# One of the gate's products done as seven smaller ones instead of eight, over two weight pairs and two token pairs, in the first two weight groups

## The chip, the cores and the metric

The kernel runs on one core of a Trainium2 chip. A run's time is the device time in microseconds (us) from launch to end. TensorE (PE in the profile, its weight loads PEld) does the matmuls, VectorE (DVE) and ScalarE (ACT) the elementwise work, GpSimd (POOL) some of it and some DMA issues, SyncE (SP) issues most DMAs. TensorE writes its sums to PSUM, which has 8 banks; a bank holds 512 fp32 numbers in each of 128 partitions.

## The reference, cut to what matters

```python
def reference(A_x, A_w1, A_b1, A_w2, A_b2, B_x, B_w_gate, B_w_up, B_w_down, gate_w):
    x = A_x                                                  # 2 x 1 x 4096 x 640
    g = sigmoid((x * gate_w).sum(-1, keepdims=True))
    a = _A_ref(x, A_w1, A_b1, A_w2, A_b2)                    # spectral mixing: rfft2, block MLP, irfft2
    b = (gelu(x @ B_w_gate) * (x @ B_w_up)) @ B_w_down       # 640 -> 1728 -> 640
    return g * a + (1 - g) * b
```

All of it is fp32. The change concerns `gelu(x @ B_w_gate) * (x @ B_w_up)`, for 8192 tokens, 640 channels and 1728 hidden columns.

## The kernel before, in words

**Precision.** Each fp32 operand is split into a high and a low part (`high` on ScalarE, `low` on VectorE), both of type float32r, and a product is three matmuls: high x high, high x low, low x high (`prod`). The helper `run` issues a list of such matmuls into one PSUM target.

**Tiling.** The hidden columns are cut into 13 full weight pairs `t` of 128 gate and 128 up columns, and a rest. The tokens are cut into 16 token pairs `tp`; each holds a first and a second half of 256 tokens. The 640 channels are a first half b1x (256, two matrices of 128), a second half b2x (256) and 128 more, k4. So `b21` is the second channel half of the first token half, and `g2` the gate's weights for the second channel half.

**The quad.** For one `tp` and one `t`, `quad` computes gate and up for both token halves with a seven-product scheme (g1 b11, g2 b21, s1 t1, s2 t2, s3 t3, s4 b22, u2 t4; t1 to t4 and s1 to s4 are sums of tokens and of weights). Its running sums: bank `X` starts with g1 b11 and is copied by ScalarE to `p1`; bank `C` takes s3 t3; bank `A` takes g2 b21, 6 matmuls, and VectorE adds it to p1 (L525), which is the gate of the first token half. X goes on with s2 t2 (copied to `u2`), and the quad's second part, three functions in the queue `Q`, runs between the products of the next quad: s1 t1 on X (`u4`, and gelu of p1 on ScalarE), s4 b22 on X (gelu to `h`), u2 t4 on C (added to u2 at L551). Then VectorE multiplies gate and up (L553, L554) and h is stored to `hD`.

**Order.** Weight pairs come in three groups: 0 to 3, 4 to 7, 8 to 13. `keys` lists (group, token pair) in the order of work, and for each key the quads of the group follow each other; in the second group token pair 0 comes fifth. `manual_schedule` keeps the order of the code on each engine. Other work is put between the products by a table: `slots[(i, q)]` is run by the `hook` calls of key number i, seven a quad, and `todo` after a quad. By it go the weights of the next group (`w_raw` loads, `w_prep` makes sums and splits), the tokens of the next key (`x_raw`, `x_prep`), and the first step of the spectral branch (`a_split`, `a_gate`, `a_step`), whose matmuls (L645) stand between those of the quads. In the first group `x_prep` makes t1 to t4 and keeps them in memory (`xD`, stored by GpSimd); in later groups they are loaded from there.

**Buffers.** Tiles come from tagged pools of fixed size (`big`, `mid`, `small`, `tiny`, 8 PSUM banks); an instruction that writes a tile waits until the slot's earlier users are done. Semaphores are set by the framework: readers and writers of one PSUM bank are kept apart whichever columns they touch.

Of the kernel before, what the change touches and what calls it, by code (L numbers as in the profile page):

```python
# [23 lines left out]
CW = CH + 2  # L24
NCH = 8
NPAIR = 13

# [186 lines left out]
def spectral_mix_kernel(ctx: ExitStack, tc: tile.TileContext, a):  # L214
# [36 lines left out]
    def st(dst, src):  # L251
        late.append((dst, src))
# [10 lines left out]
    hD = dram.tile([64, P, 14 * P], F32, name="hD")  # L263
    wdf = [dram.tile([P, 13 * 320], F32, name=f"wdf_{j}") for j in range(7)]
    wdl = dram.tile([P, 7 * 320], F32, name="wdl")

    fny = consts.tile([P, 8], F32, name="fny")
    sgn = consts.tile([P, 4], F32, name="sgn")
# [33 lines left out]


    WG, XT, XO, RAW = {}, {}, {}, {}

    def w_raw(t):
        RAW[t] = []
# [5 lines left out]
    def w_prep(t, plain=False):  # L313


        o = {}

        def gate_high():
            o["r"] = RAW.pop(t)
            o["w0"] = big([P, 5, 2, P], F32R, name="w0")  # L320
            high(o["w0"][:, :, 0], o["r"][0])

        def up_high():
            o["w1"] = big([P, 5, 2, P], F32R, name="w1")
            high(o["w1"][:, :, 0], o["r"][1])

        def up_low():
            low(o["w1"][:, :, 1], o["r"][1], o["w1"][:, :, 0])
            WG[t] = o["w0"], o["w1"]

        def st0():
            if not plain:
                gate_high()
            if t < NPAIR:
# [60 lines left out]
        def piece(ks):  # L395
            if "r" not in o:
                o["r"] = RAW.pop(t)
                o["w0"], o["w1"] = (big([P, 5, 2, P], F32R, name=f"w{k}") for k in range(2))
                WG[t] = o["w0"], o["w1"]
            for w, r in zip(WG[t], o["r"]):  # L400
                high(w[:, ks, 0], r[:, ks])
            for w, r in zip(WG[t], o["r"]):
                low(w[:, ks, 1], r[:, ks], w[:, ks, 0])
        if plain:
            if t == 0:
                return [piece, st0, st1, st3, st4, st5, st6, st7]
            return [gate_high, st2, up_high, up_low, st0, st1, st3, st4, st5, st6, st7]
        return [st0, st1, st2, st3, st4, st5, st6, st7] if t < NPAIR else [gate_high, st2]

    made = lambda key: key[0] == 0 or key == (1, 0)

    def x_raw(key, names=("b11", "b21", "b12", "b22", "k4")):
        d = XT.setdefault(key, {})
        for n in names:
            if key[0] != 1 or made(key) or n != "b12":
# [8 lines left out]
    def x_prep(key, k, eng=nc.vector):  # L426
# [35 lines left out]
        def lo():  # L462
# [7 lines left out]
        return [src, hi, lo]  # L470

    def prod(ws, x):

# [29 lines left out]
    def quad(key, t, hook):  # L503


        o, w = XO[key], WG[t]
        half = lambda: bank()[:, :256]
        T = lambda n: tiny([P, 256], name=n)
        copy = lambda d, s_: nc.scalar.activation(d, s_, AF.Copy)  # L509
        gelu = lambda d, s_: nc.scalar.activation(d, s_, AF.Gelu_apprx_tanh)  # L510
        old = Q.pop() if Q else [lambda: None] * 3

        X = half()
        run(X, prod(w["g1"], x_of(o, "b11", ("k4", 0))))
        p1 = T("p1")
# [9 lines left out]
        nc.vector.tensor_add(p1, A, p1)  # L525
        hook(3)
        run(X, prod(w["s2"], x_of(o, "t2", "t5")), first=False)
        u2 = T("u2")
        copy(u2, X)
        hook(4)  # L530
        old[1]()
        hook(5)
        old[2]()
        hook(6)
        v = {}

        def half5():
            run(X, prod(w["s1"], x_of(o, "t1", "t5")), first=False)
            u4 = v["u4"] = T("u4")
            copy(u4, X)  # L540
            gelu(p1, p1)
            nc.vector.tensor_add(u4, C, u4)  # L542

        def half3():
            run(X, prod(w["s4"], x_of(o, "b22")), first=False)
            h = v["h"] = small([P, 512], name="h")
            gelu(h[:, 256:], X)

        def half4():
            run(C, prod(w["u2"], x_of(o, "t4")), first=False)  # L550
            nc.vector.tensor_add(u2, C, u2)  # L551
            h = v["h"]
            nc.vector.tensor_mul(h[:, 256:], h[:, 256:], v["u4"])  # L553
            nc.vector.tensor_mul(h[:, :256], u2, p1)  # L554
            h_store(key[1], t, h)
        Q.append([half5, half3, half4])

    def plain(key, t, hook):

# [840 lines left out]
        spread(0, (2, 9, 16)[k - 1], w0[k][2:4])  # L1400
    for k in range(4):
        spread(*((0, 11), (0, 20), (1, 2), (1, 10))[k], w0[k][4 if k else 1:])
    for k, (l, pb) in enumerate(((1, 0), (1, 1), (2, 0), (2, 1))):
# [187 lines left out]
```

## Time and profile before

| | before |
|---|---|
| median of 3 runs | 2538.85 us (2537.32 to 2540.7) |
| the profiled execution | 2535.42 us |
| its span, first to last instruction | 2533.7 us |
| TensorE busy | 2527.2 us (100%), granted clock 1.00 |
| VectorE busy | 2052.9 us (81%) |
| ScalarE busy | 1492.7 us (59%) |
| GpSimd busy | 372.4 us (15%) |
| DMA | 483.77 MB, mean 191 GB/s |

Busy times are sums over the span; which stage they belong to is read from windows. A matmul's record overlaps the next one's, so TensorE's busy share says that it never stood idle, not that it ran at its peak. In a group's row stand: line, engine, operation, tiles as out<-in, shapes, count, then busy us and mean ns of one, then the idle time of the engine just before. In a row of the timeline stand: start, length, engine, line, operation, tiles, count, and in brackets the engine's idle time before it and what ended it.

### The profile page before, as it was taken

How to read it: one execution, taken by the hardware profiler on the slowest of the kernel's cores; microseconds unless marked ns; L12 is line 12 of the kernel's file. 1: busy time of each engine (PE TensorE's matmuls, PEld its weight loads, DVE VectorE, ACT ScalarE, POOL GpSimd, SP SyncE). 2: the span in 40 equal slices, each digit the busy share in tenths (PEclk: the TensorE clock that was granted, in tenths of full speed). 3: DMA queues.
4: the chain of work that ended last, by engine and by line, in shares of the span. 5: the costliest groups of instructions: out<-in, count | busy, mean ns of one | idle time of the engine just before them, and what ended most of it. 6: DMA issues, size and time to landing. Idle time of an engine off the chain costs nothing.

```text
span 2533.7 us, 54552 instructions
## 1 busy us (share of the span) xinstructions
PE 2527.2 (100%) x20299; PEld 2522.9 (100%) x20299; DVE 2052.9 (81%) x4218; ACT 1492.7 (59%) x3494; POOL 372.4 (15%) x379
## 2 busy tenths in 40 slices
PE   9999999999999999999999999999999999999999
PEld 9999999999999999999999999999999999999999
DVE  7878767777777767766667788888999999899998
ACT  6655555666665655655556788787644444444443
POOL 0000000000000000000003111111133333333332
PEclk9999999999999999999999999999999999999999
DMA  6566647676767677766767354548744444344432
GB/s 231 195 214 197 212 169 234 203 240 210 223 204 253 192 227 226 232 219 209 225 224 229 121 166 141 169 144 263 288 146 150 156 157 139 134 151 157 154 130 103
DMA packets 345982, 483.77 MB, mean 191 GB/s; under 512 B 24748, under 2 KB 221996, under 8 KB 345716
## 3 DMA queue, kind: packets, MB, share of 16 engines
q1 hardware_dynamic: 330884, 438.47, 54.2%
q0 software_dynamic: 14832, 41.82, 4.6%
q8 instruction: 160, 2.62, 0.4%
q14 instruction: 106, 0.87, 0.1%
HBM read 300.55 MB, written 179.64 MB: 190 GB/s over the span
## 4 chain that ended last, share of the span: by engine, by line
PE 96%; DVE 2%; DMA 1%; ACT 1%; issue 0%; SPq 0%; DVEq 0%; ACTq 0%
PE bank L483 54%; PE bank L1234 22%; PE bank L295 14%; PE bank L811 3%; PE bank L645 1%; PE bank L892 1%; PE bank L893 1%; DMA wraw<-in_wgu_dram 0%; DVE w L279 0%; DVE xo L279 0%; PE bank L894 0%; DVE xd L441 0%; DMA xraw<-in_xT_dram 0%; DVE uu L1239 0%; DVE h L554 0%
## 5 line engine op out<-in xcount | busy, mean ns | idle before, releaser
L483 PE MATMUL bank<-xo,w 128*128 128x256 f32 x11676 | 1351.0, 277 | 0.7 <-ACT u L509 0.6
L483 PEld LDWEIGHTS bank<-xo,w 128*128 128x128 f32 x11676 | 1342.2, 188 | 1.7 <-ACT u L509 1.3
L1234 PE MATMUL bank<-wx,ho 128*128 128x320 f32 x3844 | 560.6, 306 | 0.0
L1234 PEld LDWEIGHTS bank<-wx,ho 128*128 128x128 f32 x3844 | 557.1, 188 | 0.0
L509 ACT ACTIVATE u<-bank 128x256 f32<-128x256 f32 x408 | 156.6, 384 | 253.4 <-PE bank L483 248.3
L279 DVE TENSOR_TENSOR ho<-hraw,ho 128x640 fp32r<-128x640 f32 (+3 forms) x384 | 273.8, 754 | 21.4 <-ACT ho L276 18.4
L276 ACT ACTIVATE ho<-hraw 128x640 fp32r<-128x640 f32 x320 | 166.8, 571 | 91.5 <-PE bank L1234 66.0
L509 ACT ACTIVATE p<-bank 128x256 f32<-128x256 f32 x204 | 78.6, 385 | 148.4 <-PE bank L483 61.9
L279 DVE TENSOR_TENSOR xo<-xraw,xo 128x512 fp32r<-128x512 f32 x209 | 143.2, 686 | 23.9 <-ACT xo L276 23.2
L542 DVE TENSOR_TENSOR u<-bank,u 128x256 f32<-128x256 f32 x204 | 85.9, 421 | 89.2 <-ACT u L509 86.6
L279 DVE TENSOR_TENSOR xs<-xr,xs 64x640 fp32r<-64x640 f32 x128 | 104.9, 820 | 58.1 <-ACT xs L276 55.6
L295 PE MATMUL bank<-wm,h 128*128 128x320 f32 (+1 forms) x792 | 137.7, 309 | 0.0
L276 ACT ACTIVATE xo<-xraw 128x512 fp32r<-128x512 f32 x209 | 131.0, 627 | 6.1 <-DMA xraw<-in_xT_dram 4.3
L551 DVE TENSOR_TENSOR u<-bank,u 128x256 f32<-128x256 f32 x204 | 85.5, 419 | 60.0 <-PE bank L483 59.3
L647 DVE TENSOR_TENSOR as<-bank,as 64x320 f32<-64x320 f32 x256 | 113.7, 483 | 24.9 <-ACT as L646 23.7
L295 PEld LDWEIGHTS bank<-wm,h 128*128 128x128 f32 (+1 forms) x792 | 117.9, 185 | 1.4
L598 POOL MEMSET h<- 64x512 f32 x16 | 8.4, 522 | 749.8 <-PE bank L645 437.5
L483 PE MATMUL bank<-wx,ho 128*128 128x320 f32 x764 | 116.3, 307 | 0.0
L525 DVE TENSOR_TENSOR p<-bank,p 128x256 f32<-128x256 f32 x204 | 86.6, 424 | 36.5 <-PE bank L483 31.9
L483 PEld LDWEIGHTS bank<-wx,ho 128*128 128x128 f32 x764 | 112.1, 188 | 0.0
L276 ACT ACTIVATE ho<-hs 128x640 fp32r<-128x640 f32 (+1 forms) x128 | 69.0, 570 | 70.2 <-DVE ho L279 51.1
L646 ACT ACTIVATE as<-bank 64x320 f32<-64x320 f32 x256 | 96.8, 427 | 16.4 <-PE bank L645 13.9
(168 smaller groups left out, 3669.6 us busy)
## 6 DMA issues: line engine op xcount, KB each, us to landing
xo<-xD SPq DMA_DIRECT2D x124, 512.0 KB
xraw<-in_xT_dram SPq DMA_DIRECT2D x225, 256.0 KB
hD<-h SPq DMA_DIRECT2D x224, 256.0 KB
hraw<-hD SPq DMA_DIRECT2D x128, 320.0 KB
xD<-xo POOLq DMA_DIRECT2D x64, 512.0 KB, 4.3
sc<-scr SPq DMA_DIRECT2D x65, 320.0 KB
xr<-in_x_dram SPq DMA_DIRECT2D x64, 320.0 KB
scr<-as SPq DMA_DIRECT2D x64, 320.0 KB
```

The costliest lines, as they stand in the source:

```text
L276: nc.scalar.activation(dst, src, AF.Copy, scale=scale)
L279: eng.tensor_sub(dst, src, hi.bitcast(F32))
L295: nc.tensor.matmul(dst, l, r, start=i == 0, stop=i == len(ops) - 1)
L483: nc.tensor.matmul(dst, l, r, start=first and i == 0, stop=i == len(ops) - 1, skip_group_check=True)
L509: copy = lambda d, s_: nc.scalar.activation(d, s_, AF.Copy)
L525: nc.vector.tensor_add(p1, A, p1)
L542: nc.vector.tensor_add(u4, C, u4)
L551: nc.vector.tensor_add(u2, C, u2)
L646: nc.scalar.activation(stg[hi, cs], pa[lo, :320], AF.Copy)
L647: nc.vector.tensor_add(stg[hi, cs], pa[hi, :320], stg[hi, cs])
L811: nc.tensor.matmul(pz[:, kp * P:(kp + 1) * P], SC[b, c, kp][:, o:o + P], ft, start=True, stop=True)
L1234: nc.tensor.matmul((X, Y)[k], *op, start=n[k] == 0 and not (more and k), stop=n[k] == tot[k] - 1, skip_group_check=True)
```

## The change

For the token pairs 3 to 14 in the first two groups (`deep(key)`), bank A and its six matmuls leave the quad. Two weight pairs t, t+1 and two token pairs tp, tp+1 (tp odd, t even) form a block, and the four products g2 x b21 of the block are computed together, once more by a seven-product scheme: m1 to m7, each of three matmuls, on sums of weights (`w_deep`, in a tile `w4`) and sums of tokens (`x_deep`, tiles `xo` and `xs`). In the first group the split token sums are made and stored to a new memory tile `xA`; in the second they are loaded from it, and b21 is neither loaded nor split there.

The seven products run in six functions f0 to f5 (`deep_parts`), which `extra(k)` issues at four points of the three quads that follow the block's last one. One bank serves all: its left half (q = 0) and right half (q = 1) are two running sums, and after each product VectorE adds the sum so far into one of the four p1 tiles (`go`, L694). Gelu and the product with u2 move behind these adds, so p1 and u2 of the earlier quads are kept in a tile `pb`, and h of the odd token pairs is stored in two halves. The weights of the next group are loaded from (14, 1) on instead of (13, 3), and the first of them prepared at (15, 0) instead of (14, 10).

```diff
+FIRST = 3
+    def deep(key):
+        return key[0] < 2 and FIRST <= key[1] < 15
...
+    def w_deep(t):
+        def st0():
+            g, g2 = GR.pop(t), GR.pop(t + 1)
+            x = o["x"] = small([P, 4, P], name="wt")
+            nc.vector.tensor_add(x[:, 0], g2[:, 2], g2[:, 3])
+            nc.vector.tensor_sub(x[:, 2], g[:, 2], g2[:, 2])
+            nc.vector.tensor_sub(x[:, 1], x[:, 0], g[:, 2])
+            nc.vector.tensor_sub(x[:, 3], g[:, 3], x[:, 1])
...
+    def x_deep(gr, tp):
+            names = (("m1", "m2"), ("m5", "m6"), ("m3",), ("m7",), ("m4",))[k]
...
+            if gr:
+                return [lambda: ld(tile().rearrange("p h n -> p (h n)").bitcast(F32), xA[tp][:, ends])]
...
@@ def quad(key, t, hook):
         copy(p1, X)
+        extra(0)
         hook(0)
         old[0]()
         hook(1)
         C = half()
         run(C, prod(w["s3"], x_of(o, "t3", ("k4", 1))))
+        extra(1)
         hook(2)
-        A = half()
-        run(A, prod(w["g2"], x_of(o, "b21")))
-        nc.vector.tensor_add(p1, A, p1)
+        if not dp:
+            A = half()
+            run(A, prod(w["g2"], x_of(o, "b21")))
+            nc.vector.tensor_add(p1, A, p1)
         hook(3)
         run(X, prod(w["s2"], x_of(o, "t2", "t5")), first=False)
...
         copy(u2, X)
+        extra(2)
         hook(4)
         old[1]()
         hook(5)
         old[2]()
+        extra(3)
         hook(6)
...
+    def deep_parts(gr, tp, t):
+        def go(m, q, first, dst):
+            if not b:
+                b.append(bank())
+            acc = b[0][:, 256 * q:256 * q + 256]
+            for i, (l, r) in enumerate(prod([wa[m]], [xa[m]])):
+                nc.tensor.matmul(acc, l, r, start=first and i == 0, stop=i == 2, skip_group_check=True)
+            nc.vector.tensor_add(dst, acc, dst)
+        def f0():
+            go("m2", 1, True, p11)
+            go("m7", 0, True, p22)
+        def f1():
+            go("m4", 0, False, p21)
+            go("m1", 1, True, p11)
+            g11()
+        def f2():
+            e11()
+            go("m6", 1, False, p21)
+            g21()
+        def f3():
+            e21()
+            go("m5", 1, False, p22)
+            g22()
+        def f4():
+            e22()
+            go("m3", 1, False, p12)
+            g12()
...
+        E.extend([(0, f0), (2, f1), (0, f2), (1, f3), (3, f4), (0, f5)])
...
-            (i, j), (i2, s) = [((13, 3), (14, 10)), ((14, 3), (15, 8)), ((15, 0), (15, 17)), ((15, 2), (16, 4)), ((15, 3), (16, 12)), ((15, 1), (15, 25))][k]
+            (i, j), (i2, s) = [((14, 1), (15, 0)), ((14, 3), (15, 8)), ((15, 0), (15, 17)), ((15, 2), (16, 4)), ((15, 3), (16, 12)), ((15, 1), (15, 25))][k]
```

In the changed kernel `run` stands at L562, the product of a block at L693 and its add at L694. TensorE's order before, in the third quad of key 4 (first group, token pair 4): X's product, s1 t1 of the quad before, C's product, and A's six matmuls (bank_1552), each sum in a bank of its own:

```order
L483 MATMUL bank_1510<-xo_1051,w0_292 128x256 x6
L483 MATMUL bank_1510<-xo_1098,w0_292 128x256 x3
L483 MATMUL bank_1419<-xo_1269,w1_280 128x256 [waits Activation_49]
L483 MATMUL bank_1419<-xo_1269,w1_280 128x256 x5
L483 MATMUL bank_1419<-xo_463,w1_280 128x256 x3
L483 MATMUL bank_1541<-xo_1130,w2_648 128x256 [waits DVE_49]
L483 MATMUL bank_1541<-xo_1130,w2_648 128x256 x5
L483 MATMUL bank_1541<-xo_1098,w2_648 128x256 x3
L483 MATMUL bank_1552<-xo_1170,w0_292 128x256 [waits DVE_49]
L483 MATMUL bank_1552<-xo_1170,w0_292 128x256 x5
```

The two waits on VectorE there (DVE_49 is its semaphore) are for earlier users of a bank. The same place after the change, f0 of the block of token pairs 3, 4 and weight pairs 0, 1: xo_1696 holds the tokens of m1 and m2, xs_1771 those of m7, and bank_1859 is the block's bank:

```order
L562 MATMUL bank_1848<-xo_1426,w0_298 128x256 [waits PE_49]
L562 MATMUL bank_1848<-xo_1426,w0_298 128x256 x5
L562 MATMUL bank_1848<-xo_1471,w0_298 128x256 x3
L693 MATMUL bank_1859<-xo_1696,w0_158 128x256 x3
L693 MATMUL bank_1859<-xs_1771,w4_1024 128x256 [waits DVE_49]
L693 MATMUL bank_1859<-xs_1771,w4_1024 128x256 x2
L562 MATMUL bank_1759<-xo_1620,w1_286 128x256 [waits Activation_49]
```

Between X's product and s1 t1 now stand m2 and m7, and the first matmul of m7 waits for VectorE. A's six matmuls are gone from behind C's product. Later in the same quad, f1, behind s2 t2 on X: m4 and then m1, each with a wait for VectorE:

```order
L562 MATMUL bank_1848<-xo_1546,w2_654 128x256 x5
L562 MATMUL bank_1848<-xo_469,w2_654 128x256 x3
L693 MATMUL bank_1859<-xs_1808,w0_283 128x256 [waits DVE_49]
L693 MATMUL bank_1859<-xs_1808,w0_283 128x256 x2
L693 MATMUL bank_1859<-xo_1696,w0_158 128x256 [waits DVE_49]
L693 MATMUL bank_1859<-xo_1696,w0_158 128x256 x2
L562 MATMUL bank_1759<-xo_1644,w3_540 128x256 [waits Activation_49]
```

VectorE's order at the same place after the change, from the end of the second quad to the adds of f1:

```order
L650 TENSOR_TENSOR h_1724<-bank_1700,h_1724 128x256 [waits PE_49]
L651 TENSOR_TENSOR h_1724<-h_1724,u4_1783 128x256 [waits DVE_49,Activation_49]
L281 TENSOR_TENSOR xo_1833<-xd_1811,xo_1833 128x512 [waits Activation_49]
L694 TENSOR_TENSOR pb_1354<-bank_1859,pb_1354 128x256 [waits PE_49]
L694 TENSOR_TENSOR p1_1769<-bank_1859,p1_1769 128x256 [waits DMAHW6_49,PE_49]
L281 TENSOR_TENSOR xs_1843<-xraw_1335,xs_1843 128x256 [waits Activation_49]
L640 TENSOR_TENSOR u4_1879<-bank_1788,u4_1879 128x256 [waits DMAHW0_49,Activation_49]
L473 TENSOR_TENSOR xd_1882<-xraw_1661,xraw_1657 128x512
L473 TENSOR_TENSOR xd_1884<-xraw_1663,xd_1882 128x512 [waits DVE_49]
L476 TENSOR_TENSOR xd_1898<-xraw_1665 128x256
L694 TENSOR_TENSOR pb_1354<-bank_1859,pb_1354 128x256 [waits PE_49] x2
```

The first L694 is the add of m2, the second that of m7; the last row holds those of m4 and m1. Each waits for its product on TensorE, and whatever stands ahead of it in the row comes first.

More of the change, by code (lines that the diff above doesn't have):

```diff
@@ L416, in x_raw @@
         for n in names:
-            if key[0] != 1 or made(key) or n != "b12":
+            if (key[0] != 1 or made(key) or n != "b12") and not (key[0] == 1 and deep(key) and n == "b21"):
                 r = d[n] = small([P, 512], name="xraw")
@@ L469, in lo, with part, tile, hi @@
                                     XM.pop((key, name)).rearrange("p h n -> p (h n)").bitcast(F32))
-        return [src, hi, lo]
+        return [lambda: None] * 3 if name == "b21" and deep(key) else [src, hi, lo]
+    def x_deep(gr, tp):
+        o = {}
+        F = XA[gr, tp] = {}
+        def part(k):
+            names = (("m1", "m2"), ("m5", "m6"), ("m3",), ("m7",), ("m4",))[k]
+            ends = slice(*((0, 1024), (1024, 2048), (2048, 2560), (2560, 3072), (3072, 3584))[k])
+            def tile():
+                if k < 2:
+                    m = mid([P, 2, 512], F32R, name="xo")
+                else:
+                    m = small([P, 624], F32R, name="xs")[:, 112:].rearrange("p (h n) -> p h n", h=2)
+                o[k] = m
+                for j, n in enumerate(names):
+                    F[n] = tuple(m[:, h, 256 * j:256 * j + 256] for h in range(2))
+                return m
+            if gr:
+                return [lambda: ld(tile().rearrange("p h n -> p (h n)").bitcast(F32), xA[tp][:, ends])]
+            def hi():
+                high(tile()[:, 0], o["src"][k])
+            def lo():
+                m = o[k]
+                low(m[:, 1], o["src"][k], m[:, 0])
+                nc.gpsimd.dma_start(xA[tp][:, ends], m.rearrange("p h n -> p (h n)").bitcast(F32))
+            return [hi, lo]
+        def sums(k):
+            def f():
+                p, q = XT[0, tp]["b21"], XT[0, tp + 1]["b21"]
+                a_, b_ = slice(0, 256), slice(256, 512)
+                if not k:
+                    x = o["x"] = [small([P, 512], name="xd") for i in range(2)]
+                    o["src"] = [p, x[0], q[:, b_], x[1][:, a_], x[1][:, b_]]
+                    nc.vector.tensor_sub(x[0][:, a_], q[:, a_], p[:, a_])
+                    nc.vector.tensor_sub(x[1][:, a_], q[:, b_], q[:, a_])
+                else:
+                    x = o["x"]
+                    nc.vector.tensor_sub(x[0][:, b_], q[:, b_], x[0][:, a_])
+                    nc.vector.tensor_sub(x[1][:, b_], p[:, b_], x[0][:, b_])
+            return f
+        return [sums(0), sums(1)], [part(k) for k in range(5)]
     def prod(ws, x):
@@ L511, in quad @@
         old = Q.pop() if Q else [lambda: None] * 3
+        dp = deep(key)
+        ahead_ = dp and key[1] % 2 == 1
         X = half()
         run(X, prod(w["g1"], x_of(o, "b11", ("k4", 0))))
-        p1 = T("p1")
+        if ahead_:
+            if t % 2 == 0:
+                PB[t] = big([P, 5, 256], name="pb")
+            p1, u2 = (PB[t - t % 2][:, 2 * (t % 2) + k] for k in range(2))
+        elif dp and t % 2 == 0:
+            p1 = PB[t][:, 4]
+        else:
+            p1 = T("p1")
         copy(p1, X)
+        extra(0)
         hook(0)
@@ L551, in half4 @@
             nc.vector.tensor_add(u2, C, u2)
[L552 to L555, printed above, removed]
-        Q.append([half5, half3, half4])
+            nc.vector.tensor_mul(v["h2"], v["h2"], v["u4"])
+            if ahead_:
+                half_store(key[1], t, 1, v["h2"])
+            elif not dp:
+                nc.vector.tensor_mul(v["h"][:, :256], u2, p1)
+                h_store(key[1], t, v["h"])
@@ new lines, in end, with extra @@
+        def end():
+            nc.vector.tensor_mul(u2, u2, p1)
+            if ahead_:
+                half_store(key[1], t, 0, u2)
+            else:
+                h_store(key[1], t, v["h"])
+        if dp:
+            PEND[key[1], t] = p1, lambda: gelu(p1, p1), end
+        Q.append([half5, half3, half4])
+        if dp and not ahead_ and t % 2:
+            deep_parts(key[0], key[1] - 1, t - 1)
+    PB, E = {}, []
+    def extra(k):
+        while E and E[0][0] == k:
+            E.pop(0)[1]()
@@ L1402, in spectral_mix_kernel @@
         spread(*((0, 11), (0, 20), (1, 2), (1, 10))[k], w0[k][4 if k else 1:])
+    for t, i, s in ((0, 2, 1), (2, 2, 11), (4, 15, 25), (6, 16, 13)):
+        for k, f in enumerate(w_deep(t)):
+            spread(i, s + 2 * k, [f])
+    for i, (gr, tp) in enumerate(keys):
+        if deep((gr, tp)) and tp % 2:
+            p, f = x_deep(gr, tp)
+            if gr == 0:
+                spread(i, 22, p[:1])
+                spread(i, 24, p[1:])
+            for k, q in enumerate((0, 1, 3, 4, 2)):
+                if gr:
+                    spread(i, 16 + 3 * k, f[q])
+                else:
+                    spread(i + 1, 1 + 3 * k, f[q][:1])
+                    spread(i + 1, 2 + 3 * k, f[q][1:])
     for k, (l, pb) in enumerate(((1, 0), (1, 1), (2, 0), (2, 1))):
```

39 lines of the change are left out of this document (35 added, 4 removed).

## The prediction

> **What bounds the kernel now.** I read the page first, then who waited for whom on TensorE, then the windows of the two stages that the change touches, then the timeline around the few places where TensorE did wait.
>
> ```profile
> span 2533.7 us, 54552 instructions
> PE 2527.2 (100%) x20299; PEld 2522.9 (100%) x20299; DVE 2052.9 (81%) x4218; ACT 1492.7 (59%) x3494; POOL 372.4 (15%) x379
> PE 96%; DVE 2%; DMA 1%; ACT 1%; issue 0%; SPq 0%; DVEq 0%; ACTq 0%
> ...
> PE bank L1344 <- DVE zero L1340: 1.2, 1, 1.2
> PE bank L295 <- ACT is L987: 0.7, 1, 0.7
> PE bank L483 <- ACT u L509: 0.6, 2, 0.5
> ...
> 150.00:250.00 100.00, 100.00 (x878) 100.00 (x877) 78.04 (x168) 59.84 (x140) 8.50 (x16) 1.00 0.62 205
> 650.00:750.00 100.00, 100.00 (x873) 100.00 (x873) 73.52 (x164) 61.40 (x143) 0.00 (x0) 1.00 0.69 216
> ```
>
> TensorE is the bound: it holds 96% of the chain that ended last, and all its listed waits come to 2.5 us. The last two rows are windows of 100 us in the first and the second weight group (busy times of PE, PEld, DVE, ACT, POOL, then granted clock, DMA share, GB/s): TensorE has no gap at clock 1.00, VectorE is at 78 and 74%. So a matmul saved there shortens the span by its issue interval, and any wait put into TensorE's row lengthens it in full, since nothing later has slack to give it back.
>
> **Matmuls removed.** The block of two weight pairs x two token pairs needed 4 products g2 x b21 of 6 matmuls; now 7 products of 3. That is 24 - 21 = 3 matmuls a block. With t in two pairs a group, two groups and six token pairs (3,4 to 13,14) there are 2 x 2 x 6 = 24 blocks, 72 matmuls.
>
> ```profile
> 299.76 9.46 PE L483 MATMUL bank<-xo,w 128*128 128x256 f32 x82
> L483 PE MATMUL bank<-xo,w 128*128 128x256 f32 x11676 | 1351.0, 277 | 0.7 <-ACT u L509 0.6
> ```
>
> One record lasts 277 ns (second row, mean), but 82 of them fill 9.46 us: (9.46 - 0.277) / 81 = 0.1134 us from start to start. Gain: 72 x 0.1134 = 8.2 us. This is all that the change can bring: 0.32%.
>
> **The wait added.** In `deep_parts` one bank holds two running sums side by side. f0 runs m2 into its right half, lets VectorE add that half into p11 (L694), and then runs m7 into the left half. The order shows that m7's first matmul waits for VectorE, and the count that it waits for is that of the L694 add issued just before it: the two touch the same bank, though not the same columns. f1 has the same shape: m4, add, then m1. Two such waits a block, 24 blocks: 48. TensorE works in order, so behind each stands all the rest of its row. The other waits on VectorE in the block (m4, m6, m5, m3) ask for adds that 15 or more matmuls (1.7 us) separate from them; I cost these at nothing, with the 9 to 24 matmuls between as their cover.
>
> The kernel before never has this round trip, so I price its three legs from the nearest rows.
>
> ```profile
> 450.65 1.30 PE L483 MATMUL bank<-xo,w 128*128 128x256 f32 x10
> 451.98 0.38 ACT L509 ACTIVATE p<-bank 128x256 f32<-128x256 f32 x1 [1.01 <-PE bank L483]
> ...
> L525 DVE TENSOR_TENSOR p<-bank,p 128x256 f32<-128x256 f32 x204 | 86.6, 424 | 36.5 <-PE bank L483 31.9
> ...
> 51.44 0.50 PE L483 MATMUL bank<-xo,w 128*128 128x256 f32 x3
> 52.00 0.37 ACT L509 ACTIVATE u<-bank 128x256 f32<-128x256 f32 x1
> 52.42 0.86 PE L483 MATMUL bank<-xo,w 128*128 128x256 f32 x5 [0.48 <-ACT u L509]
> ```
>
> - Product's end to reader's start: 450.65 + 1.30 = 451.95 to 451.98, 0.03 us (a ScalarE reader that stood idle).
> - The add itself: 0.424 us, the mean of L525, the same add of a 128x256 half bank.
> - Reader's end to TensorE's start: 52.37 to 52.42, 0.05 us.
>
> Idle TensorE: 0.51 us, against 0.48 in the one stall of this kind that the trace has. More is lost than the idle time shows: in steady flow the next matmul starts 0.277 - 0.113 = 0.16 us before the last one ends, and after the stall at 52.42 five matmuls take 0.86 us instead of 0.277 + 4 x 0.1134 = 0.73, so 0.13 for the restart. Sum 0.51 + 0.16 + 0.13 = 0.80 us; 48 x 0.80 = 38.4 us. Bounds: without the restart 0.67 each (32.2 us); from below, nothing at all if the add were done before TensorE came; from above, VectorE comes late.
>
> The Trainium skill, PSUM — Partial Sum Buffer, section "PSUM bank collisions raise a hardware error", says that two engines must be kept apart by bank and not by address, because touching different columns of a bank still collides. By that rule the 48 waits are real and cannot be met early, and the sum holds them in full; without it the rows would allow anything from nothing up. The order of the kernel before agrees in that each sum there has a bank to itself; no run so far shows what sharing costs.
>
> **How late VectorE comes.** These rows give the pitch of its instructions.
>
> ```profile
> 124.51 0.69 DVE L441 TENSOR_TENSOR xd<-xraw,xd 128x512 f32<-128x512 f32 x1
> 125.11 0.68 DVE L279 TENSOR_TENSOR xo<-xraw,xo 128x512 fp32r<-128x512 f32 x1
> ...
> 127.05 0.43 DVE L551 TENSOR_TENSOR u<-bank,u 128x256 f32<-128x256 f32 x1
> 127.39 0.42 DVE L553 TENSOR_TENSOR h<-h,u 128x256 f32<-128x256 f32 x1
> 127.72 0.42 DVE L554 TENSOR_TENSOR h<-u,p 128x256 f32<-128x256 f32 x1
> ...
> L279 DVE TENSOR_TENSOR xs<-xr,xs 64x640 fp32r<-64x640 f32 x128 | 104.9, 820 | 58.1 <-ACT xs L276 55.6
> ...
> DVE p L525 <- PE bank L483: 31.9, 42, 0.9
> ```
>
> A 256-wide one takes 0.34 us of the queue, a 512-wide one 0.60, the 640-wide split about 0.74 (0.820 less the same overlap of 0.08). Today VectorE was there in time, and waited, at 42 of 204 of the L525 adds (last row); at the others the product was ready first, which cost nothing with a bank of its own. Counting the queue at the four kinds of places:
> - f0 in a key's third quad: since the quad before ended, an add, a multiply and a 512-wide low part (2 x 0.34 + 0.60 = 1.28 us) against 12 matmuls (1.36): in time.
> - f0 in a key's first quad: the last add and two multiplies of the block before come on top (+3 x 0.34), 2.3 us against 15 matmuls (1.7): 0.6 late, 12 places, 7.2 us.
> - f1 in the third quad: the u4 add can't run before the ScalarE copy of its product, about 2.1 us after m7 starts (12 matmuls 1.36 + 0.28 + 0.03 + 0.38); then 0.34 + 0.60 + 0.60 + 0.34 = 1.9: done at 4.0, against m4's end at 33 matmuls 3.74 plus restart and latency, 4.1: in time.
> - f1 in the first quad: in time, but with two 640-wide splits of the spectral step and one 512-wide part (4.6 against 4.1) in the first group's keys up to 11: 0.5 late, 4 places, 2 us.
>
> Together 9.2 us.
>
> **The rest, at nothing.** VectorE gains 3 adds a block (7 for 4) and, in the first group, per token pair four 256-wide sums and the wider low parts (five of 1792 columns in all for two of 1024). That is some 5.5 us on a pair of about 50, so 78% becomes about 89%; in the second group two 512-wide splits drop out (2 x 0.69) against six adds (2.5), about +2 points. ScalarE gains the same high parts and stays near 65%. GpSimd issues five more stores a token pair where its row shows 8.5 us in 100. SyncE issues five loads where it issued two, and half stores; the stage moves 216 GB/s at a DMA share of 0.69, and 1.3 MB more in 50 us adds 26 GB/s, to about 0.78. The raw weights of the next group are loaded about two quads later (14,1 for 13,3) and first used at 15,0; two quads or more (12 us) still cover that. If one of these covers is gone, the cost is that of a late load, below.
>
> **Sum.** -8.2 + 38.4 + 9.2 = +39.4 us. The profiled execution took 2535.42 us (its span 2533.7 and 1.7 around it), so 2574.8; its median companions stand 3.4 higher, at 2538.85, which gives 2578.
>
> **Rivals.**
> - *The waits cost nothing and the 72 matmuls are saved*: 2538.85 - 8.2 = 2530.6, faster. It needs each add to end within the 0.11 us in which the next matmul would start anyway, or the awaited count to belong to an earlier instruction. For it: TensorE's list above has no wait for VectorE in these stages, though every sum there is read by it. Against it: the add alone is 0.424 us, and nothing but the product just issued releases it. 0.04.
> - *VectorE falls behind*: at 89% with in-order work, each wait meets one 512-wide instruction more. 48 x (0.80 + 0.60) = 67.2, less 8.2: +59, 2598. For it: the 162 of 204 adds above that came late; against: every stall also gives VectorE 0.8 us to catch up. 0.12.
> - *A load comes late* in the second group, on top of the waits: the longest such wait so far is in the row below; six pairs x 3.1 us = 19, so 2597. 0.04.
>
> ```profile
> ACT xo L276 <- DMA xraw<-in_xT_dram: 4.3, 2, 3.1
> 1790.00:1810.00 20.00, 19.24 (x133) 18.65 (x132) 17.37 (x36) 15.84 (x36) 2.71 (x2) 1.00 0.98 352
> ```
>
> - *The clock drops behind each stall*: if the nine matmuls that follow ran at half speed, 48 x 9 x 0.1134 = 49 us more, 2627. Against it: the window above holds the longest late stall of TensorE, 0.7 us, with the granted clock at 1.00. 0.02. The Trainium skill, TensorE: Matmul & The Clock Gate, section "A second HAM failure mode: psum-queue depth-cycling", says that frequent short idle times of TensorE between groups can make its clock swing; this trace, at 1.00 throughout, speaks against it for single stalls and can't show it for frequent ones.
>
> **How the numbers follow.** The forecast has 0.78: 2578. The lower end takes the waits without restart and without lateness: 38.4 and 9.2 become 32.2, +24, 2563, rounded out to 2560. The upper end takes in the second and third rival, 2598, and a little of both, 2604. The fast rival and the clock stand outside, 0.06. A measurement of this kernel can tell about 0.2% (5 us) from no change. Slower by more: 0.78 + 0.12 + 0.04 + 0.02 = 0.96, of which I move 0.01 to within 0.2% for waits that turn out short; faster 0.04.
>
> **What would show it.** Right: TensorE waits for VectorE at L694 appear 48 times with 0.5 to 1.1 us each, 25 to 35 us in total as idle time; TensorE's matmuls number 72 fewer; the first two groups are longer by about 40 us together and the rest of the span is unchanged. Lateness: the longer waits sit in the keys' first quads. Wrong: no such group of waits, a shorter span (the fast rival); waits of TensorE on ScalarE or on a DMA at the head of the list; a granted clock under 1.00 in the two stages.

## The result, and the profile after

| | before | after |
|---|---|---|
| median of the runs | 2538.85 us | 2618.62 us (2614.82 to 2618.92) |
| ratio, 95% interval | | 1.031 [1.0295, 1.0325] |
| span of the profiled execution | 2533.7 us | 2614.9 us |

The change makes the kernel 3.1% slower. The forecast, 2578 us, had the direction and the cause, and less than half of the size; 2618.62 lies above its range. The page of the changed kernel, its span, busy times and shares of the chain:

```profile
span 2614.9 us, 54733 instructions
...
PE 2547.6 (97%) x20227; PEld 2530.5 (97%) x20227; DVE 2094.2 (80%) x4340; ACT 1491.3 (57%) x3504; POOL 389.7 (15%) x409
...
PE 84%; DVE 7%; DMA 4%; ACT 3%; issue 1%; SPq 0%; ACTq 0%; DVEq 0%
```

TensorE lost 72 matmuls (20299 to 20227), as counted. Its share of the chain fell from 96 to 84%, VectorE's rose from 2 to 7%. The two windows of the prediction, one in each weight group:

```profile
150.00:250.00 100.00, 91.09 (x777) 89.65 (x776) 78.81 (x174) 54.92 (x132) 13.42 (x25) 1.00 0.67 228
650.00:750.00 100.00, 92.57 (x781) 90.62 (x780) 68.07 (x153) 53.49 (x126) 0.00 (x0) 1.00 0.66 215
```

TensorE, without a gap there before, now stands still for 8.9 and 7.4 us of 100, while VectorE is no busier in the same time (78.04 to 78.81, and 73.52 to 68.07). The waits of TensorE by cause (us in total, times, longest):

```profile
PE bank L693 <- DVE pb L694: 55.7, 48, 3.8
PE bank L562 <- ACT pb L588: 2.5, 4, 0.6
```

The 48 forecast waits are there, at the forecast line, but with 55.7 us of idle time instead of 25 to 35: 1.16 us each. Two places of one quad show why. First f1 of the first block, where VectorE stood idle when the product came (timeline: start, length, engine, line, operation, tiles, count, idle time before):

```profile
124.81 0.50 PE L693 MATMUL bank<-xs,w 128*128 128x256 f32 x3
...
125.34 0.42 DVE L694 TENSOR_TENSOR pb<-bank,pb 128x256 f32<-128x256 f32 x1 [1.02 <-PE bank L693]
...
125.82 0.62 PE L693 MATMUL bank<-xo,w 128*128 128x256 f32 x3 [0.52 <-DVE pb L694]
```

This is the bare round trip as it was priced: 0.52 us of idle TensorE against 0.51. The shortest of the 48 waits is 0.515. Then f0 in the same quad:

```profile
117.27 0.50 PE L693 MATMUL bank<-xo,w 128*128 128x256 f32 x3
117.44 0.42 DVE L281 TENSOR_TENSOR xs<-xd,xs 128x256 fp32r<-128x256 f32 x1
...
117.89 0.42 DVE L650 TENSOR_TENSOR h<-bank,h 128x256 f32<-128x256 f32 x1
...
118.24 0.42 DVE L651 TENSOR_TENSOR h<-h,u 128x256 f32<-128x256 f32 x1
...
118.57 0.68 DVE L281 TENSOR_TENSOR xo<-xd,xo 128x512 fp32r<-128x512 f32 x1
119.17 0.42 DVE L694 TENSOR_TENSOR pb<-bank,pb 128x256 f32<-128x256 f32 x1
...
119.64 0.39 PE L693 MATMUL bank<-xs,w 128*128 128x256 f32 x1 [1.87 <-DVE pb L694]
```

m2 ends at 117.77, but its add starts at 119.17: four VectorE instructions that stand ahead in the row come first, and m7 waits 1.87 us. Behind this stall stands what the prediction gave a chance of 0.02. Two windows, before and behind the end of that stall (last columns: clock, DMA share, GB/s):

```profile
117.20:120.60 3.40, 1.53 (x14) 1.33 (x13) 2.65 (x7) 1.21 (x3) 1.09 (x2) 1.00 0.37 76
120.60:124.00 3.40, 3.40 (x19) 3.40 (x18) 2.18 (x6) 0.39 (x1) 0.54 (x1) 0.51 0.81 305
```

In the second TensorE is busy throughout, with 19 matmuls where full speed allows 30 (3.40 / 0.1134), at a granted clock of 0.51. The clock's record in the trace shows six such stretches in the first two groups, at 0.5 and each 3.413 us long (one pair back to back, from 533.6). Half of 6 x 3.413 is 10.2 us; about 1 us of that is counted twice, since TensorE stood idle for 1.9 us of the back-to-back pair anyway. The mean clock of the core says the same:

```profile
core 0: 2614.9 us, clock 0.996
```

(1 - 0.996) x 2614.9 = 10.5 us.

The span grew by 2614.9 - 2533.7 = 81.2 us. Its parts: 55.7 of idle time in the 48 waits; 48 x 0.29 = 13.9 for the lost overlap and the restart, as priced (around the 44 waits with full clock on both sides the starts of TensorE's matmuls give a mean of 0.287); 10.2 for the clock; less 8.2 for the matmuls: 71.6. Of the rest, TensorE's other idle time is 5.1 (span less busy, less the 55.7: 11.6 against 6.5 before); 4.5 us (5.5 without what is counted twice) are not assigned to a place. The loss sits where the change is: the last 12600 matmuls, which begin behind the last block, take 1646.5 us before and 1648.5 after.

### The profile page after: what moved, and what is told of

The parts are those of the page before. It is cut to its first block, busy times and chain, and to the rows that moved or that the text cites. A ratio compares the mean times of both kernels' runs of the same rounds, so it can differ in the third digit from the quotient of the medians.

```text
span 2614.9 us, 54733 instructions
## 1 busy us (share of the span) xinstructions
PE 2547.6 (97%) x20227; PEld 2530.5 (97%) x20227; DVE 2094.2 (80%) x4340; ACT 1491.3 (57%) x3504; POOL 389.7 (15%) x409
## 4 chain that ended last, share of the span: by engine, by line
PE 84%; DVE 7%; DMA 4%; ACT 3%; issue 1%; SPq 0%; ACTq 0%; DVEq 0%
PE bank L562 43%; PE bank L1403 21%; PE bank L297 13%; PE bank L980 3%; DMA xr<-in_x_dram 2%; PE bank L693 2%; DVE xo L281 1%; PE bank L814 1%; DVE pb L694 1%; DVE xs L281 1%; ACT xs L278 1%; DMA xo<-xD 1%; DMA xs<-xA 1%; PE bank L1061 1%; PE bank L1062 1%
## 5 line engine op out<-in xcount | busy, mean ns | idle before, releaser
L562 PE MATMUL bank<-xo,w 128*128 128x256 f32 x11100 | 1318.5, 278 | 4.6 <-ACT pb L588 2.5
L562 PEld LDWEIGHTS bank<-xo,w 128*128 128x128 f32 x11100 | 1297.6, 189 | 8.1 <-ACT pb L588 3.3
L281 DVE TENSOR_TENSOR ho<-hraw,ho 128x640 fp32r<-128x640 f32 (+3 forms) x384 | 263.6, 728 | 19.9 <-ACT ho L278 17.0
L588 ACT ACTIVATE u<-bank 128x256 f32<-128x256 f32 x312 | 119.6, 383 | 191.1 <-PE bank L562 184.4
L640 DVE TENSOR_TENSOR u<-bank,u 128x256 f32<-128x256 f32 x204 | 86.0, 422 | 94.5 <-ACT u L588 92.0
L281 DVE TENSOR_TENSOR xo<-xraw,xo 128x512 fp32r<-128x512 f32 x191 | 131.3, 688 | 35.0 <-ACT xo L278 33.6
L278 ACT ACTIVATE xo<-xraw 128x512 fp32r<-128x512 f32 x191 | 120.0, 628 | 5.5 <-DMA xraw<-in_xT_dram 4.2
L562 PE MATMUL bank<-wx,ho 128*128 128x320 f32 x764 | 116.6, 307 | 0.2 <-DVE ho L281 0.2
L562 PEld LDWEIGHTS bank<-wx,ho 128*128 128x128 f32 x764 | 112.1, 188 | 0.5 <-DVE ho L281 0.5
L500 POOL DMA_DIRECT2D xD<-xo x64 | 34.4, 538 | 471.7 <-DVE xo L281 375.8
L281 DVE TENSOR_TENSOR s2s<-s,s2s 128x320 fp32r<-128x320 f32 x128 | 97.4, 821 | 3.6 <-ACT s2s L278 2.6
L588 ACT ACTIVATE p<-bank 128x256 f32<-128x256 f32 x132 | 50.7, 384 | 82.6 <-DVE h L651 55.7
```

The lines of the kernel that those rows point to most:

```text
L278: nc.scalar.activation(dst, src, AF.Copy, scale=scale)
L281: eng.tensor_sub(dst, src, hi.bitcast(F32))
L500: nc.gpsimd.dma_start(xD[key[1]][:, kept], XM.pop((key, name)).rearrange("p h n -> p (h n)").bitcast(F32))
L562: nc.tensor.matmul(dst, l, r, start=first and i == 0, stop=i == len(ops) - 1, skip_group_check=True)
```

## The experiments

Theory A: the cost is the shared bank, 48 round trips in TensorE's row, stretched by VectorE's queue ahead of the adds. Theory B: the cost is the extra work on VectorE and in the transfers, and would be there with any banks. The kernel before took 2536.6 us (median) beside the first four, 2536.3 beside the next four and 2539.2 beside the last two; ratios are to it.

**A bank for each half.**

```diff
-        b = []
+        b = {}
         def go(m, q, first, dst):
-            if not b:
-                b.append(bank())
-            acc = b[0][:, 256 * q:256 * q + 256]
+            if q not in b:
+                b[q] = bank()
+            acc = b[q][:, 256 * q:256 * q + 256]
```

> The changed kernel, with the block's two running sums in two banks instead of the two halves of one; the products, the order and all elementwise work stay. Theory A (the shared bank: 48 round trips TensorE - VectorE - TensorE make the loss): the waits at the block's products go, the granted clock is 1.00, and the time falls from 2618.6 to 2530 to 2540, at or below the kernel before. Theory B (VectorE's extra sums and splits and the extra transfers make the loss, and the bank only shows it): TensorE waits elsewhere instead, and the time stays above 2570.

Measured: 2552.23 us, ratio 1.006 [1.0045, 1.0075]. The waits of TensorE:

```profile
PE bank L562 <- ACT pb L588: 6.8, 8, 1.1
PE bank L562 <- ACT p L588: 2.5, 3, 0.9
PE bank L693 <- DVE pb L694: 2.2, 2, 1.6
```

Of the 48 waits 2 are left, the half-speed stretches are none, and with them went 66 us: theory A holds for four fifths of the loss. But the time misses the expected 2530 to 2540: 15.6 us above the kernel before stay, 23.8 above what 72 matmuls less should give. The list now begins with ScalarE's copy of X (L588). One of these stalls in the timeline:

```profile
146.77 0.42 DVE L694 TENSOR_TENSOR pb<-bank,pb 128x256 f32<-128x256 f32 x1
...
147.22 0.42 ACT L589 ACTIVATE pb<-pb 128x256 f32<-128x256 f32 x1 [0.70 <-DVE pb L694]
147.54 0.37 ACT L588 ACTIVATE pb<-bank 128x256 f32<-128x256 f32 x1
...
147.96 0.50 PE L562 MATMUL bank<-xo,w 128*128 128x256 f32 x2 [0.67 <-ACT pb L588]
```

TensorE waits for the copy at 147.54, the copy stands in ScalarE's row behind the gelu at 147.22 (L589), and the gelu waits for VectorE's add of a block (146.77). The quad had 24 matmuls between X's product and the next use of X; with A's six gone there are 18.

**The gelus one point later, with two banks.**

```diff
         def f1():
             go("m4", 0, False, p21)
             go("m1", 1, True, p11)
-            g11()
         def f2():
-            e11()
+            g11()
             go("m6", 1, False, p21)
-            g21()
+            e11()
```

and so on through f5.

> The changed kernel with a bank for each half (as in the first experiment, 2552 us) and each gelu of the block issued one point later, at the head of the next function, with the multiply and store behind that function's product. If the 18 us of stalls left with two banks come from ScalarE's queue, where the copy of X stands behind a gelu that waits for VectorE's add, about 13 to 16 us of them go: 2534 to 2540, level with the kernel before or up to 0.2% under it. If they come from VectorE's or the transfers' extra load itself, the same stalls appear at other places and the time stays at 2548 to 2555.

Measured: 2531.88 us against 2536.28, ratio 0.9983 [0.9974, 0.9991]: 2 us under the expected range, and faster than the kernel before by 4.4 us of the 8.2 that the matmuls are worth. Its page, its two windows and its largest wait at a block's product:

```profile
span 2530.1 us, 54706 instructions
...
PE 2521.8 (100%) x20227; PEld 2517.0 (99%) x20227; DVE 2089.8 (83%) x4340; ACT 1490.0 (59%) x3504; POOL 388.3 (15%) x409
```

```profile
150.00:250.00 100.00, 100.00 (x879) 100.00 (x878) 87.54 (x195) 61.51 (x147) 14.03 (x27) 1.00 0.73 246
650.00:750.00 100.00, 100.00 (x870) 99.97 (x870) 76.17 (x172) 60.45 (x142) 0.00 (x0) 1.00 0.75 246
```

```profile
PE bank L693 <- DVE pb L694: 1.6, 1, 1.6
```

TensorE is again without a gap in both windows, although VectorE is busier there than in any other version (87.54 and 76.17). So theory B falls: the work that the change adds to VectorE and the transfers costs at most the missing 3.8 us once neither the bank nor ScalarE's order makes TensorE wait for it.

**The gelus one point later, with one bank.** The same edit in the changed kernel.

> The changed kernel, still with one bank, with each gelu of the block issued one point later (the second half of what brought 2552 to 2532 with two banks). If the copy behind the gelu is a cost of its own, beside the shared bank, 10 to 18 us go here too: 2600 to 2608. If TensorE's waits at the bank already give ScalarE the time that it lacks, the waits at L693 stay at about 55 us and the time changes by less than 8 us: 2611 to 2619.

Measured: 2611.51 us, ratio 1.0286 [1.0268, 1.0304].

```profile
PE bank L693 <- DVE pb L694: 55.5, 48, 3.5
```

7 us, at the edge of the second case, and the 48 waits are as before (55.5). The same edit is worth 20 us with two banks. The likely reason is that ScalarE catches up where TensorE stands still at the bank anyway: TensorE's waits for ScalarE's copies (the rows with pb and p at L562) come to 3.6 us in the changed kernel and to 9.3 with two banks. The two costs overlap and can't be read off one by one.

**m7 away from m2.** One bank, m7 moved to the next point, behind C's product and so 18 matmuls after m2; m4 and m1 still adjacent.

```diff
         def f0():
             go("m2", 1, True, p11)
+        def f0b():
             go("m7", 0, True, p22)
...
-        E.extend([(0, f0), (2, f1), ...
+        E.extend([(0, f0), (1, f0b), (2, f1), ...
```

> One bank as in the changed kernel, but in f0 the product m7 is moved behind C's product, 18 matmuls after m2, so that m2's add is done by then; f1 stays. Theory A: the 24 waits at f0 go (35.8 us of idle time in the trace, 24 x 0.29 us around them, and the halved clock, which showed after f0 waits alone, about 10 us), the 24 at f1 (19.9 us) stay: 2560 to 2575. Theory B: no change beyond 10 us, 2608 or more.

Measured: 2584.09 us, ratio 1.0189 [1.0174, 1.0204].

```profile
PE bank L693 <- DVE pb L694: 20.1, 26, 1.8
PE bank L693 <- DVE p L694: 7.9, 14, 1.3
```

Half of the shared bank's cost (34.5 of 66 us) goes without another bank, as A says, but 9 us less than expected: m4 now stands only 9 matmuls behind m7, and at 14 places it waits for m7's add (second row). Nine matmuls, 1.02 us, don't cover an add here.

**A third adjacent pair.** One bank, m5 moved directly behind m6.

```diff
             go("m6", 1, False, p21)
+            go("m5", 1, False, p22)
             g21()
```

> One bank, and m5 directly behind m6, in the same half: a third round trip in each block, 24 more, with the same work. Theory A: 24 x 0.80 to 24 x 1.45 us more, 2638 to 2654. Theory B: within 10 us of the changed kernel, since nothing is added to VectorE.

Measured: 2642.26 us, ratio 1.0416 [1.0399, 1.0434].

```profile
PE bank L693 <- DVE pb L694: 76.9, 72, 4.3
```

24 waits more cost 23.6 us, 0.98 each.

**The waits alone, in the kernel before.** A's six matmuls as two runs of three in two halves of one bank, each followed by its add, 48 times; the rest is the kernel before.

```diff
+        for k in range(2):
+            run(A[:, 256 * k:256 * k + 256], ops[3 * k:3 * k + 3])
+            nc.vector.tensor_add(p1, A[:, 256 * k:256 * k + 256], p1)
```

> The kernel before, with nothing of the change but its wait: in 48 quads (token pairs 3 to 14, t even, first two groups) g2 x b21 is done in two pieces of three matmuls in the two halves of one bank, with an add to p1 behind each. No matmul saved, 48 adds more. Theory A: 48 x 0.80 us if VectorE is in time (2577), 48 x 1.45 if it is as late as in the changed kernel (2608). Theory B: 48 adds more on VectorE, which TensorE doesn't wait for today, within 5 us of 2539.

Measured: 2671.17 us, ratio 1.0532 [1.0516, 1.0548], far above the expected range. The wait, and the mean clock:

```profile
PE bank L483 <- DVE p L528: 83.6, 47, 4.2
```

```profile
core 0: 2670.4 us, clock 0.986
```

Without any other part of the change, 48 such waits cost even more: 1.78 us each, and (1 - 0.986) x 2670.4 = 37 us lost at half speed (22 stretches). The parts come to what was measured: 83.6 of idle time, 48 x 0.29 = 13.9 and 37 make 134.5 us, and the run took 134.6 longer than the kernel before. One of the places:

```profile
100.83 0.62 PE L483 MATMUL bank<-xo,w 128*128 128x256 f32 x4
...
102.27 0.68 DVE L279 TENSOR_TENSOR xo<-xraw,xo 128x512 fp32r<-128x512 f32 x1
102.87 0.42 DVE L528 TENSOR_TENSOR p<-bank,p 128x256 f32<-128x256 f32 x1
103.34 0.90 PE L483 MATMUL bank<-xo,w 128*128 128x256 f32 x3 [1.89 <-DVE p L528]
```

The first three matmuls end at 101.45, and their add starts at 102.87, behind three 512-wide instructions (the row at 102.27 is the last of them). So the bank's round trip is the cause, and its price is set by how far behind VectorE is at that place, here further than in the changed kernel.

**TensorE kept at work in the waits.** Five extra matmuls of 256 columns into an unread bank (`fill`) between m2 and m7 and between m4 and m1.

```diff
             go("m2", 1, True, p11)
+            fill("m2")
             go("m7", 0, True, p22)
```

> The changed kernel with five extra matmuls of 256 columns, into a bank that nobody reads, between m2 and m7 and between m4 and m1: TensorE works 5 x 0.1134 = 0.57 us in each of the 48 places where it stood idle 1.16 us on average. Nothing of the result is changed; 240 matmuls are added. If the half-speed windows of the changed kernel (six of 3.41 us, about 10 us lost) come from TensorE's idle time, the filled idle time leaves none or one of them and the time falls to 2606 to 2614 us although more work is done; the waits at L694's counterpart fall to about 28 us in total. If the windows have another cause, they stay at about six and the time stays at 2618. If the filler delays the waits' end (it would have to be longer than the wait), 48 x 0.57 = 27 us come on top: 2645.

Measured: 2612.79 us, ratio 1.0297 [1.0281, 1.0313].

```profile
PE bank L693 <- DVE pb L694: 30.2, 33, 2.9
```

```profile
core 0: 2613.6 us, clock 0.999
```

240 matmuls more, and no more time: idle time at L693 falls by 25.5 us, the filler's own 27.2, and the half-speed stretches from six to one. That idle time calls the half speed is shown. What it is worth is not measured by this run: its ratio's interval overlaps that of the changed kernel, and the span is only 1.3 us shorter.

**The low parts on GpSimd.** To take VectorE's queue away from ahead of the adds.

```diff
-                    f0, f1, f2_ = x_prep(nxt, k)
+                    f0, f1, f2_ = x_prep(nxt, k, nc.gpsimd if nxt[0] < 2 else nc.vector)
```

> The changed kernel with the low parts that x_prep makes for the keys of the first two groups computed on GpSimd instead of VectorE. If the 0.64 us by which the adds come late on average (mean wait 1.16 against the bare 0.52) is VectorE's in-order queue in front of them, the mean wait falls to 0.6 to 0.8, the half-speed windows go with it, and the time falls by 20 to 30 us, to 2588 to 2600. If the lateness is not VectorE's load, the waits stay at 1.1 to 1.2 and the time at 2618. If GpSimd is too slow for these parts, new waits of TensorE on GpSimd appear and the time is above 2625.

Measured: 2649.43 us, ratio 1.0445 [1.0431, 1.046]. The time is that of the third expected case, but its sign is missing: no wait of TensorE on GpSimd appears. The waits at the block's bank grew:

```profile
PE bank L693 <- DVE pb L694: 65.3, 48, 4.6
```

The reason is not in the waits but in VectorE's durations. Groups of its instructions between 100 and 1000 us (count, busy, mean ns), first the changed kernel, then this one:

```profile
L651 DVE TENSOR_TENSOR h<-h,u 128x256 f32<-128x256 f32 x128 | 53.0, 414 | 0.0
L694 DVE TENSOR_TENSOR pb<-bank,pb 128x256 f32<-128x256 f32 x120 | 50.6, 422 | 24.8 <-PE bank L693 24.3
```

```profile
L651 DVE TENSOR_TENSOR h<-h,u 128x256 f32<-128x256 f32 x124 | 101.5, 818 | 6.4 <-ACT h L589 5.9
...
L694 DVE TENSOR_TENSOR pb<-bank,pb 128x256 f32<-128x256 f32 x120 | 50.1, 418 | 25.9 <-PE bank L693 25.5
```

The multiply of two SBUF tiles takes 818 ns instead of 414, the add with one operand in PSUM 418 instead of 422. One case in the timeline:

```profile
152.25 1.42 POOL L281 TENSOR_TENSOR xo<-xraw,xo 128x512 fp32r<-128x512 f32 x1 [6.37 <-ACT xo L278]
...
152.49 1.46 DVE L651 TENSOR_TENSOR h<-h,u 128x256 f32<-128x256 f32 x1
```

The multiply, 0.42 us elsewhere, begins while GpSimd is at work and ends 0.28 us after it. The run moved the work and slowed what stayed, so it says nothing on the theory. The Trainium skill, SBUF — State Buffer, section "Who interferes with whom", says that a VectorE instruction with two SBUF inputs contends with a GpSimd instruction that reads SBUF, and that one with at most one SBUF input doesn't, outside certain two-port modes; both rows agree.

**Without the low parts.** The same question, put another way.

```diff
-            low(t[1], XT[key][name], t[0], eng)
+            if key[0] == 2:
+                low(t[1], XT[key][name], t[0], eng)
+            else:
+                t[1] = t[0]
...
```

and alike in `x_deep`. The high part stands in for the low one, so this kernel leaves out the low part of these tokens and serves for timing alone.

> The changed kernel without the low parts of the tokens that x_prep and x_deep make for the keys of the first two groups: the matmuls take the high part in their place, so matmuls, loads and stores are as many as before, and VectorE is rid of its 512-wide subtractions ahead of the adds (the products lose their low x term). If the 0.64 us by which the adds come late is VectorE's in-order queue, the mean wait falls from 1.16 to 0.52 to 0.75 us (25 to 36 us in all), no or one half-speed window is left, and the time falls by 30 to 45 us, to 2573 to 2589, about what the prediction had with its lateness term at 0 to 9 us. If the lateness has another cause, the waits stay above 1.0 and the time above 2605.

Measured: 2595.21 us, ratio 1.0221 [1.0203, 1.0239]; 6 us above the expected range, with three half-speed stretches where one at most was expected. The waits of TensorE (L693 is L700 here), and f0 at the place shown above:

```profile
PE bank L700 <- DVE pb L701: 41.5, 48, 2.7
```

```profile
115.01 0.43 DVE L657 TENSOR_TENSOR h<-bank,h 128x256 f32<-128x256 f32 x1 [1.22 <-PE bank L569]
...
115.35 0.42 DVE L658 TENSOR_TENSOR h<-h,u 128x256 f32<-128x256 f32 x1
...
115.83 0.50 PE L700 MATMUL bank<-xo,w 128*128 128x256 f32 x3
...
116.37 0.42 DVE L701 TENSOR_TENSOR pb<-bank,pb 128x256 f32<-128x256 f32 x1 [0.60 <-PE bank L700]
...
116.85 0.62 PE L700 MATMUL bank<-xs,w 128*128 128x256 f32 x3 [0.52 <-DVE pb L701]
```

The add and the multiply of the quad before (L657, L658) are done before m2 is, the block's add follows at once, and the wait is 0.52 instead of 1.87. At the f0 of the third quads in the first group all six waits are 0.51 to 0.52. So there the lateness was these subtractions. It stays at other places, where the spectral step's 640-wide splits or the block's own multiplies are ahead, and the mean of all 48 is 0.86.

**The weights' move alone.** The kernel before with its raw weights loaded from (14, 1) and prepared at (15, 0).

```diff
-            (i, j), (i2, s) = [((13, 3), (14, 10)), ...
+            (i, j), (i2, s) = [((14, 1), (15, 0)), ...
```

> The kernel before with one part of the change alone: the first raw weights of the next group loaded from (14, 1) on and prepared at (15, 0). If this move is hidden, as the prediction had it at nothing, the time is that of the kernel before within 2 us. If the load or the preparation comes late, a wait of TensorE on weights appears at the group's start and the time is 3 to 10 us above.

Measured: 2535.5 us, ratio 0.9995 [0.9986, 1.0004]: no change.

## Why the prediction was wrong in size

**Right.** The bound; the 72 matmuls; the 48 waits, their line and their cause; the bare trip (0.515 to 0.52 of idle time against 0.51); the weights' move at nothing.

**The step that failed: "How late VectorE comes".** It gave 9.2 us; the waits hold 55.7 - 48 x 0.515 = 31.0, or 0.65 a wait. That is 21.8 of the 41.8 us by which the sum (39.4) fell short of the 81.2; the clock's 10.2 are the next part. Mean idle time of the six waits at each kind of place, from the 48 rows of m7 and m1 in the trace, with the prediction's 0.51 plus lateness beside it:

| place | predicted | first group | second group |
|---|---|---|---|
| f0, third quad | 0.51 | 1.37 | 1.78 |
| f0, first quad | 1.11 | 1.46 | 1.44 |
| f1, third quad | 0.51 | 0.64 | 0.57 |
| f1, first quad | 0.84 / 0.51 | 1.21 | 0.80 |

f1 in the third quad came out right, where the count began at an instruction that waits for a copy. f0 in the third quad, "in time", was on average 0.9 to 1.3 late, as late as in the first quads, the only places where the prediction had f0 late. In the first group two of the six waits were the bare 0.52 and four were 1.72 to 1.87. The count began at the end of the quad before, as if VectorE had no arrears then, and it left out the split of the block's own tokens (117.44 in the row above). The run without low parts shows this queue as the cause at the first group's f0. In the second group the longest of the 48 waits, 3.84 us at 535.52, has a late load in its chain:

```profile
532.15 0.74 ACT L278 ACTIVATE xs<-xr 64x640 fp32r<-64x640 f32 x1 [2.09 <-DMA xr<-in_x_dram]
...
532.92 0.82 DVE L281 TENSOR_TENSOR xs<-xr,xs 64x640 fp32r<-64x640 f32 x1 [3.13 <-ACT xs L278]
```

ScalarE waits for tokens of the spectral step (xr), VectorE for ScalarE, and the block's add behind both. The other f0 of the second group's third quads are alike: at five of the six, VectorE stood idle for 1.75 to 3.13 us until ScalarE had done its half of this split, and the block's add came behind it; the sixth, with no such split ahead, waited the bare 0.52. So there VectorE was not behind with its work; an instruction that waited for another engine stood ahead of the add, and the count had no such term. At four of the five ScalarE itself had waited for the load (0.33 to 2.09 us), so the rival "A load comes late" took part too, by way of the adds; how much of the second group's lateness is loads wasn't separated.

The rival "VectorE falls behind", with a chance of 0.12, had the size of this term: 0.60 a wait against the 0.65 measured. Its counter-argument, that every stall gives VectorE time to catch up, did not carry.

**The clock.** The rival "The clock drops behind each stall" had 0.02, since one wait of 0.7 us had left the clock at 1.00. It comes true in part: five of the 48 waits, the longest of them 3.84 us, are followed by the six stretches at half speed, 10 us. The filler run shows that idle time calls it; the row relied on was too short a stall to speak against it.

**What was put at nothing.** The block's other four products were given no wait, "with the 9 to 24 matmuls between as their cover". In the changed kernel that came out right, all 48 waits at L693 being those of m7 and m1; but nine matmuls would not have been enough, as the run with m4 nine behind m7 shows. "The rest, at nothing" had VectorE's added work about right: without the waits it is busy for 87.5 and 76.2 us of 100 (two banks, late gelus) against the stated 89 and some 76. It had no term for X's copy, which lost cover when A's matmuls left: 20 us with two banks. In the changed kernel itself this cost is mostly hidden behind the bank's waits, 7 us.

## What to carry to other kernels

Count a PSUM bank as one resource: two sums in its halves, one product directly behind the other, cost TensorE a full trip through the reader's queue, 0.8 us at best and 1.45 on average here (1.16 of idle time and 0.29 around it). With a bank for each, four fifths of the loss went; with the gelus moved behind the copies as well, the change became a small gain. Count a reader's queue from a place where it is known to be idle, not from a convenient mark in the code. When matmuls are taken out, ask what copy they had been covering, and keep instructions that wait for another engine from standing ahead of that copy.

## What the runs showed of the hardware that was not expected

- The granted clock halves for 3.413 us after a stretch of the same length in which TensorE stood idle for about half. In each trace the drops lie on one grid of 3.413 us; counted on it over these runs, the idle time in the full-speed stretch ahead of a drop was 1.78 us or more, every stretch with more than 1.92 us was followed by one, and between the two it went either way. It is the sum in the stretch that counts: in the run with m7 moved, the one drop followed 2.30 us of idle time in which no wait was longer than 1.4. The Trainium skill, TensorE: Matmul & The Clock Gate, section "What's actually happening", gives a free-running window of 3413 ns and half speed after at least one idle window; length and half speed agree, but here a window that was a little over half idle was enough.
- GpSimd at work on SBUF doubled VectorE's mean time for a multiply of two SBUF tiles (414 to 818 ns) and left the add with a PSUM operand alone (422 and 418 ns).
